# Attention and a gated feed-forward block on one core: three pairs of lag in place of two, gated tokens through DRAM, and another order at the end of a feed-forward phase

## The chip, the cores and the metric

One Trainium2 chip, of which the kernel uses one core. The engines of a core that matter here are TensorE (PE, matmuls), VectorE (DVE), ScalarE (ACT), GpSimd (POOL) and SyncE (SP), whose queue issues every DMA of this kernel. Each engine works through its own instructions in program order and waits for semaphores of the others. The metric is the device time of one execution in microseconds.

## The reference

```python
scores = np.matmul(z, z.transpose(0, 2, 1)) / S            # batch 4, S 3008, z 64 wide
attn = np.maximum(scores, 0.0) ** 2
x = (u * np.matmul(attn, v)).reshape(B * S, D)             # u, v 256 wide
rms = np.sqrt(np.mean(x * x, axis=-1, keepdims=True) + 1e-06)
xn = x / rms * rms_g
g, val = xn @ w_gate, xn @ w_val                           # 256 x 1536
return (g / (1 + np.exp(-g)) * val) @ w_out                # 1536 x 256
```

All of it is float32, and the kernel keeps that accuracy with matmuls of two halves (high and low) of each operand.

## The kernel before

The 3008 tokens of a batch are cut into 24 key tiles of 128 (the last of 64) and 6 query chunks of 512 (the last of 448). Two query chunks make a pair, so there are 3 pairs in a batch and 12 in all. For each pair p there are two phases:

- **Attention phase A(p)**, `phase_a`: 24 steps, one for each key tile. A step has up to 4 score matmuls (lines 366 and 367, high and low half of the moving operand), the relu on ACT (line 371) and the product with the score on DVE (line 373), which gives relu squared, then the high half H on ACT (line 389), the low half L on DVE (line 392) and 12 matmuls with v (lines 431, 432, 436). For some steps, the "squares" of `is_square`, ACT squares and DVE does nothing. Score tiles that a later pair needs transposed are stored as halves (line 411) and reloaded as T (line 344). At the end of the phase the gate multiplies the result by u (line 454), in place in the tile ux, into which u was loaded (line 446).
- **Feed-forward phase M(p)**, `phase_m` and `Unit`: 12 units. The gate and value products are computed as seven products of 3 matmuls (lines 616 to 618) with combined weights wu, which `load_unit` reloads from DRAM for every pair (line 600, a ring of 6 buffers). The unit's additions, silu and products follow on ACT and DVE (lines 623 to 710), the last of them, line 710, gives s. Its high and low halves hH (line 628, ACT) and hL (line 633, DVE) go into the output products py (lines 644, 645, 648), of which each unit has one for each of its two halves, `y(0)` and `y(1)`. Three such pieces of PE work wait at any time in the queue `pend`, and a unit takes two of them and adds two. `Unit.tail` ends a phase.

Between the two lie the norm of the gated tokens (`norm_jobs`, 23 small jobs) and the split of xn and its sums into halves (`split_jobs`, tiles xh and xl). The order of the phases was

```python
# before: A0 A1 M0 A2 M1 A3 M2 ... A11 M10 M11
```

Which other work runs beside a phase is set by a table: `at(phase, slot, fn)` puts a function into a slot (an attention phase has 24, one for each step; a feed-forward phase 36, three for each unit), `hook` calls it there, and `Beside.put` looks for the next slot with room on the engine. Such work is

- the weights, once: each third j is decoded on DVE and ACT (lines 142 to 153), combined in pieces of 128 columns on POOL (lines 124, 168, 169), and stored to DRAM as wc. j = 0 ran in A0, j = 1 in A1, j = 2 and half of w_out in M0;
- each batch b after the first (`plan_batch`): loads of z and v, high halves of v on ACT (line 301), low halves of v on POOL (line 312). It ran in M1, M4 and M7, before the batch's first attention phase;
- the moving operand of the next attention phase (`prep_mov`): a load of zT into a "raw" buffer (line 249), and its halves mh and ml on DVE (lines 254 and 255).

SP issues all DMAs in program order from one queue.

Of the kernel before, what the change touches and what calls it, by code (L numbers as in the profile page):

```python
# [19 lines left out]
P = 128  # L20
# [10 lines left out]
def kernel(  # L31
# [31 lines left out]
    LA = 2  # L63
    PIECE = 128
# [26 lines left out]
    misc = const.tile([P, 2 * P], F32, name="misc")  # L91
    g_sb, warm = misc[:, :ND], misc[:, ND:ND + 1]
# [80 lines left out]
    def prep_proj(j, pool, tags):  # L173
# [57 lines left out]
        "batch": ["raw", "mh0", "raw", "ml0", "mh1", "ml1"],  # L231
# [121 lines left out]
    def emit_s(p, i):  # L353
        b, c0 = where(p)[:2]
        kt = order(p)[i]
        todo = []
        for k in range(2):
# [10 lines left out]
            todo.append((k, n, ps))  # L368
        for k, n, ps in todo:
            a = att[p, i, k] = work.tile([P, CH], F32, tag="r", name="r", bufs=6)  # L370
            nc.scalar.activation(a[:, :n], ps[:, :n], AF.Relu)  # L371
            if not is_square(p, i, k):
                nc.vector.tensor_tensor(a[:, :n], ps[:, :n], a[:, :n], op=ALU.mult)  # L373

    copies = [0]

    def emit_l(p, i):
        b, c0 = where(p)[:2]
        kt = order(p)[i]
        for k in range(2):  # L380
# [61 lines left out]
    def load_u(p):  # L442
        t0, n2 = where(p)[2:]
        for d in range(ND):
            t = work.tile([P, PAIR], F32, tag=f"ux{d}", name=f"ux{d}")
            nc.sync.dma_start(out=t[:, :n2], in_=uT[d * P:(d + 1) * P, t0:t0 + n2])
            ux[p, d] = t
# [10 lines left out]
    def norm_jobs(p):  # L458
# [4 lines left out]
        small = misc[:, P:].rearrange("p (k a) -> p k a", a=PAIR // BLK)  # L463
# [100 lines left out]
    def split_jobs(p):  # L564
        n = where(p)[3] // 2
        last = p == NPAIR - 1
# [40 lines left out]
    class Unit:  # L607
# [108 lines left out]
        def tail(self, fills):  # L716

            fills = deque(fills)
            self.end0()
            if fills:  # L720
                fills.popleft()()
            self.end1()
            self.end2()
            pend.popleft()()
            if fills:
                fills.popleft()()
            self.end3()
            while pend:
                pend.popleft()()
# [87 lines left out]
    for p in range(NPAIR):  # L817
# [4 lines left out]
        for i in range(0, NK, 2):  # L822
            for k in range(2):
                if is_turned(p, i, k):
                    go = lambda p=p, i=i, k=k: load_turned(p, i, k)
                    if i < 8 and p > 1:
                        at(("M", p - 2), 3 * (NF - 2 if i < 6 else NF - 1) + 1, go)
                    else:
                        at(ph, max(i - 7, 0), go)
        if p:  # L830
            for f in range(ahead(p - 1)):
                at(ph, NK - 3 + f, lambda p=p, f=f: load_unit(p - 1, f))
        at(ph, 1 if p == 0 else (23 if p == 1 else 10), lambda p=p: load_u(p))
        if 0 < p < NPAIR:
            for i in range(NO):
                s = 19 + i * 4 // NO if p == 1 else i
                one = lambda p=p, i=i: splits(p - 1)[i][0]()
                two = lambda p=p, i=i: splits(p - 1)[i][1]()
                at(ph, s, one)
                at(ph, s + 1 if s < NK - 1 else s, two)  # L840

    def plan_batch(b):

        m = beside[b * NP - 2]
        todo = [prep_stat(b, c) for c in range(NC)] + [prep_v(b, g) for g in range(NK // 2)]
        done = []
        for k, (load, one, two) in enumerate(todo):
            if k == NC:
                m.put(norm_plan(b * NP - 1), 1)
# [10 lines left out]

    for p in range(1, NPAIR):

        m = beside[p - 1]
        if p % NP == NP - 1 and p < NPAIR - 1:
            continue
        h = m.put(norm_plan(p), 1)
        if p == NPAIR - 1:
            for i in range(NO):
                m.put([
                    ("a", 0.6, 0, lambda p=p, i=i: splits(p)[i][0]()),  # L870
                    ("d", 0.7, 0, lambda p=p, i=i: splits(p)[i][1]()),
                ], max(h, 18))
    for i, (e, cost, gap, fn) in enumerate(norm_plan(0)):
        at(("A", 1), 1 + i * 17 // 23 + (2 if i >= 8 else 0) - (1 if i < 8 else 0), fn)

    for p in range(1, NPAIR):

        for k in range(2):
            load, split, _ = prep_mov(p, k)
            if p > 1:  # L880
                m = beside[p - 2]
                at(m.phase, 3 * 9 + 1 + k, load)
                at(m.phase, 3 * 10 + 2 + k, split)
            else:
                at(("A", 0), NK - 4, load)
                at(("A", 0), NK - 1, split)
# [21 lines left out]
    tags_x = [f"xh{k}" for k in range(4)], [f"xl{k}" for k in range(4)]  # L908
    tags_m = ["mh0", "ml0", "mh1", "ml1"]

    def plan_part(part, phase, load_at, s):
# [6 lines left out]
    def plan_ends(ends, phase, s, gap=1):  # L918
        for k, fns in enumerate(ends):
            for fn in fns:  # L920
                at(phase, s + gap * k, fn)

    for j, ph, tags, s in ((0, ("A", 0), tags_x[0], 5), (1, ("A", 1), tags_x[1], 2)):
        parts, ends = prep_proj(j, moving, tags)
        for k, part in enumerate(parts):
            plan_part(part, ph, s + 2 * k - 2, s + 2 * k)
        plan_ends(ends, ph, s + 9)
# [81 lines left out]
```

## Time and profile before

| what | value |
|---|---|
| median of 3 runs | 2170.81 us (2168.62 to 2171.17) |
| the profiled execution | 2173.18 us |
| its span, first to last instruction | 2171.4 us |
| PE busy | 2066.8 us, 95% of the span |
| DVE busy | 1614.9 us, 74% |
| ACT busy | 1433.0 us, 66% |
| POOL busy | 207.9 us, 10% |
| granted clock of PE, mean | 0.98 |
| DMA | 295.85 MB, 136 GB/s |

Busy is the time in which an engine executes an instruction. A row of idle time names what ended it, the releaser: "PE ps L616 <- DVE s L710" is PE at line 616 standing until DVE's line 710 was done. The clock of PE has two levels, 1.2 and 2.4 GHz; a granted clock of 1.00 means 2.4 GHz throughout.

### The profile page before, as it was taken

Reading aid. Unit: us, or ns where it says so; the run is one execution under the profiler, and the core shown is the slowest. Engines: PE = TensorE matmul, PEld = TensorE weight load, DVE = VectorE, ACT = ScalarE, POOL = GpSimd, SP = SyncE. Lnnn points to the kernel's source line nnn. Section 1 sums busy time; section 2 is a strip of 40 time slices with the busy share of each in tenths; the row PEclk is TensorE's granted clock in tenths of the full one; section 3 lists DMA queues with packets and bytes.
Section 4 is the critical chain, followed back from the end, with each engine's and each line's share of the span. In section 5 each row is a group of like instructions: output and inputs, shape, how many; then the busy total and the mean of one; then the engine's idle time right before and its main releaser. Section 6 shows DMA issues by size and latency. Waiting matters only on the chain.

```text
span 2171.4 us, 27099 instructions
## 1 busy us (share of the span) xinstructions
PE 2066.8 (95%) x8968; PEld 1696.4 (78%) x8968; DVE 1614.9 (74%) x2661; ACT 1433.0 (66%) x2573; POOL 207.9 (10%) x376
## 2 busy tenths in 40 slices
PE   8898869998999999999899999999899999999999
PEld 7676657886888878787688778788688877878887
DVE  8898857677877677667778768757787767776765
ACT  7787536575965775656776775656596567565665
POOL 0635440022000000003000000001300000000000
PEclk9999979999999999999999999999999999999999
DMA  4405442251544544764254553495245445375342
GB/s 132 135 23 161 141 137 69 101 173 66 181 149 124 137 155 131 169 184 136 86 193 136 144 156 118 121 191 187 87 149 165 145 114 163 129 150 151 121 154 86
DMA packets 306829, 295.85 MB, mean 136 GB/s; under 512 B 195200, under 2 KB 232192, under 8 KB 306688
## 3 DMA queue, kind: packets, MB, share of 16 engines
q1 hardware_dynamic: 306688, 294.12, 45.3%
q8 instruction: 70, 1.15, 0.2%
q14 instruction: 71, 0.58, 0.1%
HBM read 178.46 MB, written 69.47 MB: 114 GB/s over the span
## 4 chain that ended last, share of the span: by engine, by line
PE 78%; issue 7%; DVE 7%; ACT 4%; POOL 4%; DMA 2%; POOLq 0%; DVEq 0%; SPq 0%; ACTq 0%
PE po L431 11%; PE po L432 11%; PE po L436 11%; PE ps L616 8%; PE ps L618 8%; PE ps L617 8%; PE py L648 4%; PE py L644 4%; PE py L645 4%; PE ps L367 4%; PE ps L366 4%; POOL vl L312 3%; DVE hL L633 1%; ACT r L371 1%; DVE L L392 1%
## 5 line engine op out<-in xcount | busy, mean ns | idle before, releaser
L431 PE MATMUL po<-H,vh 128*128 128x512 f32 (+1 forms) x1152 | 450.9, 391 | 7.8 <-ACT H L389 4.4
L432 PE MATMUL po<-H,vl 128*128 128x512 f32 (+1 forms) x1152 | 448.9, 390 | 0.0
L616 PE MATMUL ps<-xh,wu 128*128 128x512 f32 (+1 forms) x1008 | 398.0, 395 | 36.0 <-DVE s L710 19.8
L623 ACT COPY s<-ps 128x512 f32<-128x512 f32 (+1 forms) x432 | 249.4, 577 | 227.4 <-PE ps L618 227.4
L617 PE MATMUL ps<-xh,wu 128*128 128x512 f32 (+1 forms) x1008 | 392.3, 389 | 3.6 <-DMA wu<-wc 3.6
L618 PE MATMUL ps<-xl,wu 128*128 128x512 f32 (+1 forms) x1008 | 391.7, 389 | 0.0
L436 PE MATMUL po<-L,vh 128*128 128x512 f32 (+1 forms) x1104 | 340.4, 390 | 2.6 <-DVE L L392 2.4
L373 DVE TENSOR_TENSOR r<-ps,r 128x512 f32<-128x512 f32 x356 | 231.1, 680 | 141.0 <-ACT r L371 140.5
L628 ACT CAST hH<-s 128x512 fp32r<-128x512 f32 (+1 forms) x288 | 176.6, 613 | 238.2 <-DVE s L710 222.1
L371 ACT ACTIVATE r<-ps 128x512 f32<-128x512 f32 (+1 forms) x392 | 216.0, 598 | 141.0 <-PE ps L367 129.4
L392 DVE TENSOR_TENSOR L<-r,H 128x512 fp32r<-128x512 f32 x368 | 251.7, 696 | 45.5 <-ACT H L389 41.6
L633 DVE TENSOR_TENSOR hL<-s,hH 128x512 fp32r<-128x512 f32 (+1 forms) x288 | 198.4, 689 | 104.1 <-ACT hH L628 92.8
L431 PEld LDWEIGHTS po<-H,vh 128*128 128x128 f32 x1152 | 219.8, 191 | 56.0 <-ACT H L389 6.6
L616 PEld LDWEIGHTS ps<-xh,wu 128*128 128x128 f32 x1008 | 190.8, 189 | 89.0 <-DVE s L710 26.1
L432 PEld LDWEIGHTS po<-H,vl 128*128 128x128 f32 x1152 | 219.2, 190 | 42.4
L436 PEld LDWEIGHTS po<-L,vh 128*128 128x128 f32 x1104 | 208.3, 190 | 47.4 <-DVE L L392 8.3
L644 PE MATMUL py<-hH,woh 128*128 128x512 f32 (+1 forms) x576 | 226.2, 393 | 1.2 <-ACT hH L628 1.0
L645 PE MATMUL py<-hH,wol 128*128 128x512 f32 (+1 forms) x576 | 224.9, 390 | 0.0
L617 PEld LDWEIGHTS ps<-xh,wu 128*128 128x128 f32 x1008 | 191.2, 190 | 38.8 <-DMA wu<-wc 4.7
L618 PEld LDWEIGHTS ps<-xl,wu 128*128 128x128 f32 x1008 | 191.2, 190 | 37.0
L389 ACT CAST H<-r 128x512 fp32r<-128x512 f32 x356 | 217.4, 627 | 0.2 <-DVE r L373 0.2
L648 PE MATMUL py<-hL,woh 128*128 128x512 f32 (+1 forms) x576 | 180.1, 394 | 31.2 <-DVE hL L633 31.2
(82 smaller groups left out, 2790.3 us busy)
## 6 DMA issues: line engine op xcount, KB each, us to landing
wu<-wc SPq DMA_DIRECT2D x288, 448.0 KB, 3.9
kept<-halves SPq DMA_DIRECT2D x168, 256.0 KB, 2.0
raw<-in_v SPq DMA_DIRECT2D x44, 256.0 KB, 4.1
raw<-in_zT SPq DMA_DIRECT2D x38, 256.0 KB, 4.3
ux<-in_uT SPq DMA_DIRECT2D x16, 512.0 KB, 4.7
out_T<-y SPq DMA_DIRECT2D x32, 256.0 KB, 2.0
wc<-wohi SPq DMA_DIRECT2D x21, 256.0 KB, 2.4
wc<-wolo SPq DMA_DIRECT2D x21, 256.0 KB, 2.2
```

The source lines that it names most:

```text
L371: nc.scalar.activation(a[:, :n], ps[:, :n], AF.Relu)
L392: nc.vector.tensor_tensor(lo[:, :n], a[:, :n], f32(hi[:, :n]), op=ALU.subtract)
L431: nc.tensor.matmul(po[d][:, :n], wh[:, j, ds], hi[:, :n], start=(i == 0), stop=False)
L432: nc.tensor.matmul(po[d][:, :n], wl[:, j, ds], hi[:, :n], start=False, stop=(ends and lo is None))
L436: nc.tensor.matmul(po[d][:, :n], wh[:, j, ds], lo[:, :n], start=False, stop=ends)
L616: nc.tensor.matmul(ps[:, :n], wh[:, o, :], xh[:, :n], start=start, stop=False, skip_group_check=True)
L617: nc.tensor.matmul(ps[:, :n], wl[:, o, :], xh[:, :n], start=False, stop=False, skip_group_check=True)
L618: nc.tensor.matmul(ps[:, :n], wh[:, o, :], xl[:, :n], start=False, stop=stop, skip_group_check=True)
L623: nc.scalar.copy(s, ps[:, :self.n])
L644: nc.tensor.matmul(acc[h, d][:, :n], woh[:, f, ds], hi[:, :n], start=(f == 0), stop=False)
L645: nc.tensor.matmul(acc[h, d][:, :n], wol[:, f, ds], hi[:, :n], start=False, stop=False)
L648: nc.tensor.matmul(acc[h, d][:, :n], woh[:, f, ds], lo[:, :n], start=False, stop=(f == NF - 1))
```

## The change

- The order of the phases becomes A0 A1 A2 M0 A3 M1 ... A11 M8 M9 M10 M11 (`LAG = 3`).
- The gate leaves ux: four pieces of u are loaded in the last three steps of A(p) into buffers of other tiles, multiplied (line 475), stored to a DRAM tile xg (line 476), and loaded again by `load_x` (line 488) into ux, in step 9 of A(p+1) for most pairs.
- The preparation of all weights is spread over A0, A1 and A2. Its loads run 3 steps ahead instead of 2.
- `is_square` changes: 12, 12 and 6 steps' halves in pairs 0, 1 and 2, in place of 12, 24 and none.
- Batch preparation moves to M0, M3 and M6, and the norms and splits move with the order. The ring of buffers of batch loads begins with the four tiles of the moving operand.
- `emit_s` is cut into `s_product`, `s_relu` and `s_mult`, and `tail` puts these of the next pair's steps 0 and 1 between the last output products.

The core of the diff; cut are the plans of norms and splits, `load_u`, and the loop that calls the phases:

```diff
     raws = {
...
-        "batch": ["raw", "mh0", "raw", "ml0", "mh1", "ml1"],
+        "batch": ["mh0", "ml0", "mh1", "ml1", "raw", "raw"],
...
     def is_square(p, i, k):
-        if p == 0:
-            return (2 * i + k) % 4 == 1
-        return p == 1 and k == 1
+        return p < 3 and k == 1 and i % 4 in ((1, 3), (1, 3), (2,))[p] and not is_turned(p, i, k)
...
     def emit_gate(p, k):
+
         n = width(where(p)[1] + k)
-        cs = slice(k * CH, k * CH + n)
+        if p not in xg:
+            xg[p] = dram.tile([ND, P, PAIR], F32, tag=f"xg{p}", name=f"xg{p}")
         for d in range(ND):
-            x = ux[p, d]
-            nc.vector.tensor_tensor(x[:, cs], acc[k, d][:, :n], x[:, cs], op=ALU.mult)
+            x = us.pop((p, k, d))
+            nc.vector.tensor_tensor(x[:, :n], acc[k, d][:, :n], x[:, :n], op=ALU.mult)
+            nc.sync.dma_start(out=xg[p][d, :, k * CH:k * CH + n], in_=x[:, :n])
+
+    def load_x(p):
+        n2 = where(p)[3]
+        for d in range(ND):
+            t = ux[p, d] = work.tile([P, PAIR], F32, tag=f"ux{d}", name=f"ux{d}")
+            nc.sync.dma_start(out=t[:, :n2], in_=xg[p][d, :, :n2])
...
-        def tail(self, fills):
-
-            fills = deque(fills)
+        def tail(self, q=None):
+
             self.end0()
-            if fills:
-                fills.popleft()()
+            if q is not None:
+                s_product(q, 0)
             self.end1()
+            if q is not None:
+                s_relu(q, 0, 0)
             self.end2()
             pend.popleft()()
-            if fills:
-                fills.popleft()()
+            if q is not None:
+                s_relu(q, 0, 1)
+                s_mult(q, 0, 0)
             self.end3()
-            while pend:
-                pend.popleft()()
+            if q is not None:
+                s_mult(q, 0, 1)
+                emit_l(q, 0, (0,))
+            pend.popleft()()
+            if q is not None:
+                emit_s(q, 1)
+                emit_l(q, 0, (1,))
+            pend.popleft()()
+            assert not pend
...
+        at(ph, NK - 3, lambda p=p: load_u(p, [(0, 0)]))
+        at(ph, NK - 1, lambda p=p: load_u(p, [(0, 1), (1, 0), (1, 1)]))
...
-        m = beside[b * NP - 2]
+        m = beside[(b - 1) * NP]
...
+    def plan_part(part, g):
         load, upper, lower, split = part
-        at(phase, load_at, load)
-        at(phase, s, upper)
-        at(phase, s + 1, lower)
-        at(phase, s + 2, split)
...
+        at_step(g - 3, load)
+        at_step(g, upper)
+        at_step(g + 1, lower)
+        at_step(g + 2, split)
+
+    for j, steps, end in ((0, (5, 9, 13, 17), 26), (1, (24, 28, 32, 36), 39), (2, (40, 44, 48, 51), 54)):
+        parts, ends = prep_proj(j, moving, tags_w[j])
+        for g, part in zip(steps, parts):
+            plan_part(part, g)
+        for k, fns in zip((0, 1, 2, 3, 5, 7, 8, 10, 12), ends):
             for fn in fns:
-                at(phase, s + gap * k, fn)
...
+                at_step(end + k, fn)
+    for f, g in zip(range(0, NF, 2), (54, 57, 60, 63, 66, 69)):
+        plan_part(prep_wout(f), g)
```

How the order moves at three places. First DVE at the end of M1, before: s and r are the last unit's and the next attention phase's tiles, hL the low half that the output products wait for, py the outputs.

```order
L710 TENSOR_TENSOR s<-ps,s 128x512
L665 TENSOR_TENSOR s<-ps,s 128x512
L373 TENSOR_TENSOR r<-ps,r 128x512 x2
L633 TENSOR_TENSOR hL<-s,hH 128x512
L672 TENSOR_TENSOR s<-s 128x512
L373 TENSOR_TENSOR r<-ps,r 128x512 x2
L392 TENSOR_TENSOR L<-r,H 128x512 x2
L633 TENSOR_TENSOR hL<-s,hH 128x512
L656 COPY y<-py 128x512 x2
```

And after (line 661 is hL, 381 the score product, 406 L, 684 the copy of an output):

```order
L738 TENSOR_TENSOR s<-ps,s 128x512
L693 TENSOR_TENSOR s<-ps,s 128x512
L661 TENSOR_TENSOR hL<-s,hH 128x512
L700 TENSOR_TENSOR s<-s 128x512
L381 TENSOR_TENSOR r<-ps,r 128x512
L661 TENSOR_TENSOR hL<-s,hH 128x512
L381 TENSOR_TENSOR r<-ps,r 128x512
L406 TENSOR_TENSOR L<-r,H 128x512
L684 COPY y<-py 128x512
L381 TENSOR_TENSOR r<-ps,r 128x512 x2
L406 TENSOR_TENSOR L<-r,H 128x512
L684 COPY y<-py 128x512
```

The second hL now stands behind one score product, where it stood behind four and two L; the copies of the outputs lie between score products and L.

Second PE at the same place, before: the end of an output product, the scores of step 1 (lines 366 and 367), and the first of the last unit's two output products.

```order
L648 MATMUL py<-hL,woh 128x512 x2
L366 MATMUL ps<-mh,zst_4107 128x512
L367 MATMUL ps<-ml,zst_4107 128x512
L366 MATMUL ps<-mh,zst_4107 128x512
L367 MATMUL ps<-ml,zst_4107 128x512
L644 MATMUL py<-hH,woh 128x512
L645 MATMUL py<-hH,wol 128x512
L644 MATMUL py<-hH,woh 128x512
L645 MATMUL py<-hH,wol 128x512
L648 MATMUL py<-hL,woh 128x512 x2
```

And after:

```order
L676 MATMUL py<-hL,woh 128x512 x2
L366 MATMUL ps<-mh,zst_3370 128x512
L367 MATMUL ps<-ml,zst_3370 128x512
L366 MATMUL ps<-mh,zst_3370 128x512
L367 MATMUL ps<-ml,zst_3370 128x512
L672 MATMUL py<-hH,woh 128x512
L673 MATMUL py<-hH,wol 128x512
L672 MATMUL py<-hH,woh 128x512
L673 MATMUL py<-hH,wol 128x512
L676 MATMUL py<-hL,woh 128x512 x2
```

The scores of step 1 moved behind the first output product of the last unit, and lie between the two.

Third SP's queue of DMAs at the end of A4 and in the next feed-forward phase, before: stores of kept halves, then weights of all 12 units.

```order
L411 DMA kept_7223<-halves 128x1024
L411 DMA kept_7215<-halves 64x1024
L411 DMA kept_7223<-halves 64x1024
L600 DMA wu<-wc_80 128x896 x8
L600 DMA wu<-wc_81 128x896 x8
L600 DMA wu<-wc_82 128x896 x8
```

And after (line 628 loads weights, 465 a piece of u, 476 stores gated tokens):

```order
L425 DMA kept_6419<-halves 64x1024
L425 DMA kept_6427<-halves 64x1024
L628 DMA wu<-wc_80 128x896 x2
L465 DMA u<-in_uT 128x512
L628 DMA wu<-wc_80 128x896 x4
L465 DMA u<-in_uT 128x512 x3
L476 DMA xg_6700<-u 128x512 x2
L628 DMA wu<-wc_80 128x896 x2
L476 DMA xg_6700<-u 128x512 x2
L628 DMA wu<-wc_81 128x896 x8
L628 DMA wu<-wc_82 128x896 x8
```

The u pieces and the stores of the gated tokens now stand between the loads of the first weights; before, u was loaded in step 10 of the phase.

## Rows read from the trace of the kernel before

Names: ps scores or products in PSUM, po attention output, py feed-forward output, wu combined weights, s a unit's values, hL its low half, ml and vl low halves of the moving operand and of v, r relu and its square, H and L its halves.

**Rows 1.** The page, part 1: busy us (share of the span) xinstructions
```profile
PE 2066.8 (95%) x8968; PEld 1696.4 (78%) x8968; DVE 1614.9 (74%) x2661; ACT 1433.0 (66%) x2573; POOL 207.9 (10%) x376
```

**Rows 2.** Windows: us, busy of PE, PEld, DVE, ACT, POOL, PEclk, DMA, GB/s
```profile
5.50:197.00 191.50, 179.00 (x744) 140.87 (x745) 168.65 (x266) 150.31 (x279) 82.25 (x136) 0.99 0.34 106
197.00:334.80 137.80, 107.20 (x400) 81.88 (x399) 98.82 (x161) 64.97 (x120) 52.12 (x92) 0.87 0.41 133
334.80:421.60 86.80, 83.89 (x373) 71.62 (x372) 62.94 (x106) 56.49 (x108) 0.00 (x0) 0.96 0.23 72
421.60:515.10 93.50, 90.89 (x399) 74.24 (x398) 70.26 (x116) 62.29 (x115) 23.46 (x46) 1.00 0.45 150
...
1300.90:1391.70 90.80, 90.62 (x400) 74.35 (x400) 68.57 (x117) 53.34 (x97) 0.00 (x0) 1.00 0.44 127
```

**Rows 3.** Waits of PE, whole span: total us, times, longest
```profile
PE py L648 <- DVE hL L633: 31.2, 13, 3.1
```

**Rows 4.** Waits of PE in 197 to 334.8 us
```profile
PE ps L616 <- DVE s L710: 13.0, 6, 4.9
PE ps L616 <- DMA wu<-wc: 12.3, 2, 8.0
```

**Rows 5.** Timeline 874 to 881.5: start, us, engine line op, idle before and releaser
```profile
875.15 0.68 DVE L672 TENSOR_TENSOR s<-s 128x512 f32<-128x512 f32 x1
...
877.02 1.22 DVE L373 TENSOR_TENSOR r<-ps,r 128x512 f32<-128x512 f32 x2 [1.19 <-ACT r L371]
...
878.16 0.68 DVE L392 TENSOR_TENSOR L<-r,H 128x512 fp32r<-128x512 f32 x1
...
879.91 0.68 DVE L633 TENSOR_TENSOR hL<-s,hH 128x512 fp32r<-128x512 f32 x1
...
880.65 0.73 PE L648 MATMUL py<-hL,woh 128*128 128x512 f32 x2 [2.91 <-DVE hL L633]
```

**Rows 6.** Windows of 10 us behind two of the ten changes
```profile
340.00:350.00 10.00, 7.09 (x21) 5.49 (x20) 6.70 (x11) 6.79 (x12) 0.00 (x0) 0.66 0.41 158
1919.00:1929.00 10.00, 7.09 (x26) 5.88 (x26) 6.28 (x12) 7.00 (x13) 0.00 (x0) 0.83 0.42 160
```

**Rows 7.** Waits of DVE, whole span
```profile
DVE ml L255 <- POOL vl L312: 16.4, 6, 4.3
```

**Rows 8.** Timeline 504 to 521, a split on DVE
```profile
516.13 0.69 DVE L255 SCALAR_TENSOR_TENSOR ml<-raw,mh 128x512 fp32r<-128x512 f32 x1 [4.27 <-POOL vl L312]
```

**Rows 9.** Lines of DVE in 197 to 334.8: xcount | busy, mean ns | idle before
```profile
L145 DVE SCALAR_TENSOR_TENSOR wraw<-wraw,wt 128x512 uint32<-128x512 uint32 x7 | 5.0, 710 | 8.8 <-ACT w L142 5.2 <-ACT woh L142 3.7
...
L143 DVE TENSOR_SCALAR wt<-wraw 128x512 uint32<-128x512 uint32 x7 | 3.5, 505 | 0.0
...
L454 DVE TENSOR_TENSOR ux<-po,ux 128x512 f32<-128x512 f32 x4 | 2.7, 687 | 3.5 <-DMA ux<-in_uT 3.4
```

**Rows 10.** Window 150 to 195 us
```profile
150.00:195.00 45.00, 40.78 (x180) 33.29 (x179) 39.25 (x64) 36.56 (x68) 31.28 (x48) 1.00 0.39 115
```

**Rows 11.** Lines of DVE in 150 to 195 us
```profile
L392 DVE TENSOR_TENSOR L<-r,H 128x512 fp32r<-128x512 f32 x20 | 15.8, 804 | 2.6 <-ACT r L387 2.0 <-PE po L436 0.3 <-ACT H L389 0.2
L373 DVE TENSOR_TENSOR r<-ps,r 128x512 f32<-128x512 f32 x12 | 8.1, 676 | 0.2 <-ACT r L371 0.2
```

**Rows 12.** Lines of DVE in 540 to 609 us
```profile
L392 DVE TENSOR_TENSOR L<-r,H 128x512 fp32r<-128x512 f32 x36 | 24.4, 684 | 3.6 <-ACT H L389 3.6
```

**Rows 13.** Lines of POOL, whole span
```profile
L124 POOL TENSOR_TENSOR wolo<-w,wohi 128x128 fp32r<-128x128 f32 x60 | 36.2, 633 | 27.5 <-ACT wohi L195 10.3 <-issue 9.1 <-DMA wc<-wohi 7.9
```

**Rows 14.** DMA issues: out<-in, queue, kind, xcount, KB each, us to landing
```profile
ux<-in_uT SPq DMA_DIRECT2D x16, 512.0 KB, 4.7
out_T<-y SPq DMA_DIRECT2D x32, 256.0 KB, 2.0
```

**Rows 15.** Timeline 779 to 789, SP's queue and DVE
```profile
781.10 7.89 SPq L600 DMA_DIRECT2D wu<-wc  x2
...
787.42 1.28 DVE L454 TENSOR_TENSOR ux<-po,ux 128x512 f32<-128x512 f32 x2
```

More of the change, by code (lines that the diff above doesn't have):

```diff
@@ L825, with plan_splits, split_jobs_at @@
                     go = lambda p=p, i=i, k=k: load_turned(p, i, k)
-                    if i < 8 and p > 1:
-                        at(("M", p - 2), 3 * (NF - 2 if i < 6 else NF - 1) + 1, go)
+                    if i < 8 and p >= LAG:
+                        at(("M", p - LAG), 3 * (NF - 2 if i < 6 else NF - 1) + 1, go)
                     else:
                         at(ph, max(i - 7, 0), go)
[L830 to L840, printed above, removed]
+        if p >= LAG - 1:
+            for f in range(ahead(p - LAG + 1)):
+                at(ph, NK - 3 + f, lambda p=p, f=f: load_unit(p - LAG + 1, f))
+        at(ph, NK - 3, lambda p=p: load_u(p, [(0, 0)]))
+        at(ph, NK - 1, lambda p=p: load_u(p, [(0, 1), (1, 0), (1, 1)]))
+    def plan_splits(p, phase, slots):
+        for (one, two), s in zip(split_jobs_at(p), slots):
+            at(phase, s, one)
+            at(phase, s + 1 if s < NK - 1 else s, two)
+    def split_jobs_at(p):
+        return [
+            (lambda i=i: splits(p)[i][0](), lambda i=i: splits(p)[i][1]()) for i in range(NO)
+        ]
     def plan_batch(b):
-        m = beside[b * NP - 2]
+        m = beside[(b - 1) * NP]
         todo = [prep_stat(b, c) for c in range(NC)] + [prep_v(b, g) for g in range(NK // 2)]
@@ L847, in plan_batch @@
         for k, (load, one, two) in enumerate(todo):
-            if k == NC:
-                m.put(norm_plan(b * NP - 1), 1)
+            if k == NC and b == 1:
+                m.put(norm_plan(1), 1)
             s = max(3 * (k // 2) - 2, 0) + k % 2
@@ L859 @@
         plan_batch(b)
-    for p in range(1, NPAIR):
-        m = beside[p - 1]
[L864 to L874, printed above, removed]
+    at(("A", 1), 3, lambda: load_x(0))
+    for i, (e, cost, gap, fn) in enumerate(norm_plan(0)):
+        at(("A", 1), 5 + i * 15 // 23 + (2 if i >= 8 else 0), fn)
+    plan_splits(0, ("A", 2), [16, 17, 18, 19, 20, 21, 22])
+    at(("A", 2), NK - 1, lambda: load_x(1))
+    for p in range(1, NPAIR):
+        if 1 < p < NPAIR - 1:
+            at(("A", p + 1), 9, lambda p=p: load_x(p))
+        if p < NPAIR - 2:
+            plan_splits(p, ("A", p + 2), range(NO))
+        if p == 1:
+            continue
+        jobs_ = norm_plan(p)
+        m = beside[p - 1]
+        start = 1
+        if p % NP == 1:
+            early = 13
+            for i, (e, cost, gap, fn) in enumerate(jobs_[:early]):
+                at(("A", p + 1), 11 + i * 9 // early + (2 if i >= 8 else 0) + (1 if i >= 9 else 0), fn)
+            jobs_ = jobs_[early:]
+        elif p == NPAIR - 1:
+            at(m.phase, 0, lambda p=p: load_x(p))
+            start = 3
+        h = m.put(jobs_, start)
+        if p >= NPAIR - 2:
+            for one, two in split_jobs_at(p):
+                m.put([("a", 0.6, 0, one), ("d", 0.7, 0, two)], max(h, 15))
     for p in range(1, NPAIR):
@@ L884 @@
             else:
-                at(("A", 0), NK - 4, load)
-                at(("A", 0), NK - 1, split)
+                at(("A", p - 1), NK - 5, load)
+                at(("A", p - 1), NK - 1, split)
     first = {}
@@ L957 @@
         emit_l(0, 0)
-        phase_a(0)
-        for go in enter_a(1):
-            go()
-            pend.popleft()()
-        pend.popleft()()
-        phase_a(1)
+        for p in range(LAG):
+            phase_a(p)
+            if p + 1 < LAG:
+                for go in enter_a(p + 1):
+                    go()
+                    pend.popleft()()
+                pend.popleft()()
         prev = None
@@ L973 @@
                     load_unit(p + 1, f)
-        prev.tail([])
+        prev.tail()
         assert not jobs, jobs
```

81 lines of the change are left out of this document (40 added, 41 removed).

## Prediction, written before the changed kernel was run

> **What bounds the kernel now.** I read the page first: TensorE (PE) is busy for 95% of a span of 2171.4 us and VectorE (DVE) for 74% [rows 1]. So the time is PE's work plus the places in which PE stands. Then I cut the span at the first matmul of each phase and read busy time and granted clock per stretch, and after that asked for the waits of PE and of DVE. Where nothing is waited for, a matmul over 512 columns follows the last one after 0.227 us: the multiplication phase of pair 6 takes 90.8 us for 400 matmuls, with PE busy for 90.62 [rows 2] (the last row). Time is lost in three kinds of place:
>
> 1. The multiplication phase of pair 0 takes 137.8 us, with PE busy for 107.2 at a clock of 0.87 [rows 2] (the second row). It runs beside the preparation of the last third of the weights; PE waits there 13.0 us for DVE's last operation of a unit and 12.3 us, in two waits, for combined weights [rows 4].
> 2. Each of the ten changes from a multiplication phase to an attention phase. One wait is named there: the low half of the last unit (hL), made by DVE, 31.2 us in 13 waits, none over 3.1 [rows 3]. The timeline of one such tail shows why [rows 5]: the product of line 672 starts at 875.15, but the hL that needs it starts only at 879.91, behind two score multiplications and both L operations of the first attention step, since DVE works in program order. PE gets it at 880.65, after 2.91 us of standing. PE's clock then falls to half for some us: of the ten windows of 10 us behind these waits the first has a granted clock of 0.66 and the last 0.83 [rows 6], and what lacks to 1.00 adds up over the ten to 19.7 us at most.
> 3. The stretch ahead of each new batch: on DVE the split of the next moving operand (line 255) waits for GpSimd (POOL) to finish low halves of v, 16.4 us in 6 waits for the three batches [rows 7]. The operand comes through the raw buffer that POOL still reads [rows 8]: DVE stands 4.27 us.
>
> **The change part by part.** The sum is made against the profiled execution (2173.2 us, span 2171.4), which lies 2.4 above the median of the runs (2170.8).
>
> *Weights prepared in three attention phases and no multiplication phase.* The multiplication phase of pair 0 now has the batch preparation that pair 1's had, 93.5 us, and pair 1's has none, 90.8 [rows 2]. Before, the two took 137.8 + 93.5 = 231.3; after, 184.3: **−47**. Less if only the named waits went (13.0 + 12.3): −25.
>
> *What this puts into the first three attention phases.* They have 191.5 + 86.8 = 278.3 us, in which DVE is busy for 168.65 + 62.94 = 231.6, and the third has no POOL work at all [rows 2]. About 35 decoding operations of DVE at 0.50 to 0.71 us [rows 9] come in, 23 us; 6 score multiplications more, since squares go from 36 to 30, 4 us; and the price of POOL beside DVE. In a stretch of 45 us with 64 operations of DVE and 48 of POOL, POOL being busy for 31.28 [rows 10], an L operation took 804 ns and a score multiplication 676 [rows 11]; in a stretch without POOL the L operation took 684 [rows 12]. So 120 ns more for those that take both inputs from SBUF; if that is about half of the 64, 32 × 120 ns over 48 is some 70 to 80 ns per POOL operation. 84 come in: 6 us. Sum 265 of 278, 95%. In the first two phases DVE is busy for 88% and PE stands for 12.5 of 191.5 us [rows 2]; at the same share the third would stand 5.7, and I add 2 for the fuller DVE: **+8**. Bounds: −4 (loads a step earlier help the first phase) and +22.
>
> The Trainium skill has a rule that speaks against this part (SBUF — State Buffer, SBUF: two separate sides): GpSimd and VectorE share a port pair as an exclusive lock, so that a VectorE operation with two inputs in SBUF and a GpSimd operation that reads SBUF fully block one another. By it the sum would be that of the third rival. The trace shows a slowdown here, 120 ns for the L operation [rows 11, 12], and not the length of a whole POOL instruction, 633 ns [rows 13].
>
> *The tail.* On DVE hL of both halves now stands ahead of all but one score multiplication. In durations of [rows 5]: from the first score matmul on, add, hL, product, one score multiplication and hL, 5 × 0.6, and some 0.7 for casts that are waited for: ready at 3.7 us. PE needs it behind 24 matmuls (4 + 6 + 6 + 4 + 4), as many as before: 5.4 us. The wait ends: 31.2 less its three small ones, **−30**; and with it the low clock, for which I take **−15** of the 19.7, since part of those windows is the standing itself. Late next is the last copy of an output: DVE's twelfth operation there, done at 12 × 0.6 + 0.7 = 7.9 us, and PE wants that bank for the second pair of attention products, behind 36 matmuls, at 8.2. That margin is smaller than one operation; I put **+5** for the nine tails (0.5 each). Bounds for the tails in all: −17 and −50.
>
> *Batches.* Preparation moves to the multiplication phases of pairs 0, 3 and 6, which again lie right ahead of the batch's first attention, and the ring of buffers for it begins with the four of the moving operands (mh, ml), with raw last. In batches 2 and 3 the moving operands' loads then stand clear of POOL's last pieces: 5.5 us of DVE each [rows 7], **−11** (bound 0). In batch 1 the load waits for a raw buffer that POOL reads to the end, lands some 4 us later, and the split is in order on DVE ahead of the unit's additions: **+3** (0 to +8).
>
> *Gate through DRAM.* For each pair four loads of 256 KB in place of two of 512, four stores of 256 KB and two loads of 512. The DMA share is 0.44 in the undisturbed phase [rows 2], a load of 512 KB lands in 4.7 us and a store of 256 in 2.0 [rows 14], and the reload stands several steps ahead of its use: 0, with idle DMA engines as cover. The stores stand in SP's queue behind the gate, with weight loads behind them: 0, as those are needed three units later. The point to watch are the u pieces, which stand behind the weight loads that start at 781.10 and come up to 1.6 us later; 4.7 after that they are there, at 786 to 787.4. The gate starts at 787.42 [rows 15]. Just in time: 0, bounded by the fourth rival.
>
> **Sum**: −47 + 8 − 30 − 15 + 5 − 11 + 3 = −87: 2173.2 − 87 = 2086 on the profile's basis, less 2.4: **2084 us**.
>
> **Rivals.**
> *Tails half gone.* PE still stands at the nine tails, for the bank of an output that is copied late or for L of step 0, which now comes behind hL. For it: each operation put ahead pushes another back, and the margin above is 0.3 us. Against: what is late next is late by less than an operation of 0.7. Half of 45 stays: 2084 + 22 = 2106.
> *Upper bounds.* All of the clock back, −4 in the first phases, tails with no new wait: 2084 − 5 − 12 − 5 = 2062.
> *Three attention phases bound by DVE.* If each of the 84 POOL pieces held DVE for its whole length, about 0.6 us [rows 13], that would be 50 us in place of 6: 309 us of DVE. Without any idleness the three phases take 309, at the 92% of the forecast (265 of 286) 336; in the middle 322, 36 beyond the forecast: 2120. This is what the named page's rule would do here. Against it are the 804 ns of [rows 11].
> *Slower: u lands late.* DVE is in order, so a gate that waits for its DMA holds the next unit's additions, and PE follows. Once it is seen: in the multiplication phase of pair 0 the gate waited 3.4 us for u [rows 9]. Price: 12 × what the gate waits. It decides above 87/12 = 7.3 us each; at 9.4, two landings of 4.7, it is 2084 + 113 = 2197. Against: the queue ahead of the pieces is one landing long in [rows 15], not three.
>
> **Numbers.** Forecast 0.55, with a range of its own from 2068 to 2100; tails half gone 0.22; bound by DVE 0.15; u late 0.04; upper bounds 0.04. From **2060 to 2118** lie 8 in 10: outside are the last rival, most of the third and the edges. 0.2% is 4.3 us, about what a measurement of this kernel tells from no change. Between the cases at 2120 and 2197 lies little: faster 0.95, same 0.02, slower 0.03.
>
> **What would show it.** Right: the multiplication phase of pair 0 takes 91 to 100 us; no wait of PE for hL at the tails and a clock of 1.00 behind them; the third attention phase takes 87 to 95 us with DVE busy for over 85%; DVE waits for POOL or a load of raw ahead of batch 1 alone. Wrong: L operations over 1 us on the mean in the third attention phase; gate operations that wait for u; PE standing for a copy of y at the start of the attention products; any one new wait of over 20 us in all.

## The result and the profile after

The changed kernel takes 2100.2 us (median of 4 runs, 2098.6 to 2102.8) against 2171.0 before: a ratio of 0.9677, with a 95% interval of 0.9660 to 0.9694. The forecast was 2084, the range 2060 to 2118. So the direction and most of the size came as forecast, and 16 us of the gain are missing. Of the signs that the prediction named, one failed: M0 takes 111.8 us and not 91 to 100. The profiled execution has a span of 2101.0 us, 70.4 less than before. On the page after, the engines' busy time answers to [rows 1]:

```profile
PE 2041.3 (97%) x8968; PEld 1687.7 (80%) x8968; DVE 1618.2 (77%) x2668; ACT 1426.3 (68%) x2566; POOL 219.9 (10%) x376
```

The phases again from first matmul to first matmul, as in [rows 2] (us, busy time and instructions of PE, PEld, DVE, ACT and POOL, PE's clock, DMA share, GB/s): the three first attention phases, M0, A3, M1 and A5.

```profile
5.50:286.90 281.40, 263.36 (x1116) 212.22 (x1116) 259.98 (x408) 207.37 (x387) 139.97 (x220) 0.98 0.39 119
286.90:398.70 111.80, 97.19 (x398) 78.62 (x399) 79.19 (x130) 64.33 (x119) 27.16 (x55) 0.91 0.50 166
398.70:483.60 84.90, 84.84 (x373) 69.69 (x372) 74.49 (x121) 75.27 (x126) 1.49 (x3) 1.00 0.50 173
483.60:574.30 90.70, 90.54 (x399) 74.35 (x398) 68.05 (x117) 53.10 (x97) 0.00 (x0) 1.00 0.51 148
...
739.90:814.20 74.30, 70.28 (x311) 59.85 (x310) 49.17 (x90) 43.97 (x80) 0.00 (x0) 0.95 0.67 167
```

A3 and M1 have no hole left. M0 and A5 have: 111.8 us with PE busy for 97.2, and 74.3 with 70.3. Cut in the same way over both traces, the 70.4 us come from these phases:

| phases | before | after | difference |
|---|---|---|---|
| A0, A1, A2 | 278.5 | 281.4 | +2.9 |
| M0, M1 | 231.2 | 202.5 | −28.7 |
| A3, A6, A9 | 283.1 | 254.2 | −28.9 |
| A4, A7, A10 | 250.3 | 238.2 | −12.1 |
| A5, A8, A11 | 216.8 | 219.5 | +2.7 |
| M2 to M11 | 906.0 | 899.7 | −6.3 |

The waits of PE over the whole span (total us, times, longest) tell what stands in place of [rows 3] and [rows 4]:

```profile
PE ps L644 <- DMA wu<-wc: 12.0, 2, 10.5
PE po L445 <- ACT H L403: 10.5, 3, 3.8
PE po L450 <- DVE L L406: 7.6, 8, 1.8
...
PE ps L645 <- DMA wu<-wc: 3.0, 2, 2.0
...
PE ps L644 <- DVE s L738: 1.0, 1, 1.0
PE po L445 <- DVE u L475: 0.9, 2, 0.5
```

The wait for hL, 31.2 us before, is gone. New are one wait of 10.5 us for weights and three of up to 3.8 for H, and these two are what the forecast had not seen. The wait for L, 2.4 us before, is 7.6, all of it in the three first attention phases. The gate (line 475) cost PE 0.9 us in two waits, and none of them was for u.

**The tail.** The timeline at the end of M2, to be read against [rows 5]:

```profile
741.43 0.66 DVE L700 TENSOR_TENSOR s<-s 128x480 f32<-128x480 f32 x1
...
742.00 0.69 DVE L381 TENSOR_TENSOR r<-ps,r 128x512 f32<-128x512 f32 x1
...
742.75 0.66 DVE L661 TENSOR_TENSOR hL<-s,hH 128x480 fp32r<-128x480 f32 x1
...
745.10 0.59 PE L676 MATMUL py<-hL,woh 128*128 128x480 f32 x2
...
747.35 0.66 DVE L684 COPY y<-py 128x480 f32<-128x480 f32 x1
...
748.18 0.37 PE L445 MATMUL po<-H,vh 128*128 128x448 f32 x1
```

hL starts 1.3 us after the product, where it took 4.8 before, and is done 1.7 us before PE uses it. The last copy of y is done at 748.01, 0.17 us before the last of these attention products starts: the thin margin of the prediction (0.3 us) held. And the clock stays at 1.00 behind the tails, where [rows 6] had 0.66 and 0.83; a window behind the tail of M7:

```profile
1589.00:1599.00 10.00, 10.00 (x46) 8.26 (x45) 8.47 (x14) 9.82 (x18) 0.00 (x0) 1.00 0.52 180
```

**The end of M0.** Here POOL, SP's queue, DVE and PE, in order of time:

```profile
375.40 3.48 POOL L313 TENSOR_TENSOR vl<-raw,vh 128x128 fp32r<-128x128 f32 x8 [3.01 <-ACT vh L302]
378.90 4.31 SPq L250 DMA_DIRECT2D raw<-in_zT  x2
381.64 0.43 DVE L255 TENSOR_SCALAR mh<-raw 128x512 fp32r<-128x512 f32 x1 [5.96 <-DMA raw<-in_zT]
...
383.26 0.91 SPq L628 DMA_DIRECT2D wu<-wc  x2
...
386.83 0.80 PE L644 MATMUL ps<-xh,wu 128*128 128x512 f32 x1 [10.50 <-DMA wu<-wc]
```

The load of the moving operand waits for POOL, which reads the raw buffer until 378.88. Behind that load in SP's queue stand the weights of unit 11, and they go out at 383.26. PE stands for 10.5 us, and its next matmuls take 0.80 us in place of 0.39.

**A5.** SP's queue, ACT and PE:

```profile
763.71 13.18 SPq L345 DMA_TRANSPOSE T<-kept  x6
776.95 1.06 SPq L482 DMA_DIRECT2D ux<-xg  x2
782.32 0.63 ACT L504 ACTIVATE q<-ux 128x512 f32<-128x512 f32 x1 [7.46 <-DMA ux<-xg]
...
784.75 0.80 PE L445 MATMUL po<-H,vh 128*128 128x512 f32 x1 [3.66 <-ACT H L403]
```

The reload of the gated tokens is in step 9, but transposing loads stand ahead of it in the queue, and it is issued only at 776.95. The norm begins in step 11: ACT waits 7.46 us for its first operand, with the casts of H queued behind it, and PE stands for 3.66 us. A8 and A11 show the same waits (ACT 6.99 and 7.71 us, PE 3.1 and 3.8). In A5 the granted clock was 0.54 from 784 to 791; behind the wait of A8 it stayed at 1.00, and A8 is the shortest of the three (71.5 us against 74.3 and 73.7). The window of A5:

```profile
784.00:791.00 7.00, 6.25 (x17) 5.24 (x18) 5.58 (x10) 4.91 (x10) 0.00 (x0) 0.54 0.68 139
```

### The profile page after: what moved, and what is told of

Same layout as the page of the kernel before. It is cut to its first block, busy times and chain, and to the rows that moved or that the text cites. A ratio compares the mean times of both kernels' runs of the same rounds, so it can differ in the third digit from the quotient of the medians.

```text
span 2101.0 us, 27215 instructions
## 1 busy us (share of the span) xinstructions
PE 2041.3 (97%) x8968; PEld 1687.7 (80%) x8968; DVE 1618.2 (77%) x2668; ACT 1426.3 (68%) x2566; POOL 219.9 (10%) x376
## 4 chain that ended last, share of the span: by engine, by line
PE 81%; DVE 7%; issue 4%; ACT 3%; DMA 3%; POOL 1%; SPq 0%; DVEq 0%; ACTq 0%; POOLq 0%
PE po L445 11%; PE po L446 10%; PE po L450 10%; PE ps L644 10%; PE ps L645 9%; PE ps L646 9%; PE py L672 5%; PE py L673 5%; PE py L676 5%; PE ps L367 4%; PE ps L366 3%; DVE L L406 2%; DVE r L381 1%; POOL vl L313 1%; DMA ux<-xg 1%
## 5 line engine op out<-in xcount | busy, mean ns | idle before, releaser
L445 PE MATMUL po<-H,vh 128*128 128x512 f32 (+1 forms) x1152 | 452.1, 392 | 17.8 <-ACT H L403 10.5
L381 DVE TENSOR_TENSOR r<-ps,r 128x512 f32<-128x512 f32 (+1 forms) x363 | 235.5, 679 | 94.0 <-ACT r L374 93.1
L406 DVE TENSOR_TENSOR L<-r,H 128x512 fp32r<-128x512 f32 x368 | 256.6, 710 | 35.2 <-ACT H L403 32.1
L445 PEld LDWEIGHTS po<-H,vh 128*128 128x128 f32 x1152 | 219.0, 190 | 70.4 <-ACT H L403 13.1
L403 ACT CAST H<-r 128x512 fp32r<-128x512 f32 (+1 forms) x363 | 221.9, 631 | 5.1 <-DVE r L381 5.1
L313 POOL TENSOR_TENSOR vl<-raw,vh 128x128 fp32r<-128x128 f32 x144 | 75.5, 560 | 1022.7 <-ACT vh L302 1022.7
```

What stands on the lines that cost most here:

```text
L403: nc.scalar.copy(hi[:, :n], a[:, :n])
L406: nc.vector.tensor_tensor(lo[:, :n], a[:, :n], f32(hi[:, :n]), op=ALU.subtract)
L445: nc.tensor.matmul(po[d][:, :n], wh[:, j, ds], hi[:, :n], start=(i == 0), stop=False)
```

## The experiments

Each is the changed kernel with one edit unless it says otherwise; its time stands against 2100.2. The ratios to before of ahead3, ringA, woutm0, defer, oldsq and piece256 have intervals that overlap the changed kernel's (0.9660 to 0.9694), so none of these six differs from it by more than the noise, and what they teach is read from their traces. In the diffs, "..." stands for lines that are left out.

**The tail, both ways.** oldtail puts `tail` of before back; newtail is the kernel before with the new `tail` alone.

```diff
...
-                prev.tail(p + LAG)
+                prev.tail(enter_a(p + LAG))
...
```

> The changed kernel with the tail of before: hL of the last unit stands behind the score products and L of step 0 again. Theory: at each of nine tails PE stands for 3 us and then has a low clock for some us, 5 to 5.5 us each: 2145 to 2150, with a wait of PE for hL of 26 to 28 us. Rival: most of what the attention phases gained came from elsewhere (the batch order, the norm and splits that moved): 2115 to 2130.

> The kernel before with the new tail and nothing else. Theory: the ten tails lose 5 us each less: 2118 to 2126, with no wait of PE for hL at the tails and a granted clock of 1.00 behind most of them. Rival: ahead of each batch the splits wait for POOL as before, and at the three tails there PE stands for ml or s instead; at the others half of the wait moves to the copy of the outputs: 2140 to 2150.

Measured: oldtail 2142.4 (2136.9 to 2150.2), 42 more; newtail 2121.7, ratio 0.9783 (0.9768 to 0.9799), 47 less than the 2168.5 of before measured beside it. The first line is a wait of PE in oldtail, the next two are waits of PE in newtail, and the last two are windows of newtail over A4 and A5, where before had 84.6 and 72.0 us.

```profile
PE py L676 <- DVE hL L661: 27.3, 9, 3.1
```

```profile
PE py L659 <- ACT hH L643: 6.8, 3, 2.3
...
PE ps L368 <- DVE ml L255: 2.7, 3, 0.9
```

```profile
683.20:761.60 78.40, 77.61 (x341) 63.32 (x340) 56.46 (x90) 65.02 (x108) 0.00 (x0) 1.00 0.55 160
...
852.30:920.50 68.20, 67.88 (x310) 57.63 (x310) 45.37 (x74) 42.28 (x76) 0.00 (x0) 1.00 0.82 178
```

Ten tails gave 47 us, 4.7 each, and nine taken back cost 42, 4.7 each. The new tail is 42 to 47 of the 71 us that the whole change brought. Both edits exchange the whole tail, so that the order on PE and ACT moves with that on DVE; no run changes the order of DVE alone. The rival of oldtail falls, though its time is also 2.6 us below its theory's range and its four runs scatter over 13 us. Of newtail's rival the mechanism came in part: at the three tails ahead of a new batch PE stood for 2.3 us each for the high half hH and 0.9 for ml. Its price did not come, as the time lies within the theory's range.

**The norm three steps later.**

```diff
-                at(("A", p + 1), 11 + i * 9 // early + (2 if i >= 8 else 0) + (1 if i >= 9 else 0), fn)
+                at(("A", p + 1), 14 + i * 7 // early + (2 if i >= 8 else 0) + (1 if i >= 9 else 0), fn)
```

> The changed kernel with the norm of pairs 4, 7 and 10 begun in step 14 of the attention phase instead of step 11. Theory: the gated tokens land 5 to 7 us after their load is issued, the norm's first job on ACT waits for them, and the casts of H queue behind it in ACT's order. Some 9 us later they are there: the three waits of PE for H (10.5 us in all) and the low clock behind them go, A5, A8 and A11 take 67 to 69 us in place of 71.5 to 74.3, the whole 2084 to 2089. Rival: the norm's jobs now crowd the last steps of the phase, and what is gained is lost there: 2096 to 2102.

Measured: 2082.9, ratio to before 0.960 (0.9584 to 0.9616, clear of the changed kernel's 0.9677): 17 us less. The wait for H is not among its waits any more, and A5 takes 67.8 us. A window of 69 us around it:

```profile
739.00:808.00 69.00, 68.66 (x317) 58.90 (x316) 49.09 (x83) 44.07 (x80) 0.00 (x0) 1.00 0.79 181
```

A8 and A11 take 67.8 us as well. The theory holds, with its number.

**The end of M0, in three ways.** ahead3 loads the weights of pair 0 three units ahead; ringA gives the last v pieces of batch 1 other buffers; m0end lets three jobs share a slot of ACT in M0, so that v is done earlier, and puts the operand's load and split two slots later, behind the weights.

```diff
-        return 3 if p else 2
+        return 3
```

> The changed kernel with one number changed: the weights of pair 0 are loaded three units ahead, as for the other pairs, instead of two. Theory: at the end of M0 the load of the moving operand waits in SP's queue for POOL, and the weights of unit 11 wait behind it, which is PE's wait of 10.5 us. With the weights ahead of it in the queue that wait is gone: M0 goes from 111.8 to 99 to 103 us, the whole to 2088 to 2092. Rival: DVE's own wait for that operand (5.96 us, in order ahead of the unit's additions) is what holds PE, and the weights only come last: M0 stays at 105 to 109, the whole at 2094 to 2098.

```diff
+        "batch1": ["mh0", "ml0", "mh1", "ml1", "raw", "raw"] * 2 + ['mh0', 'raw', 'ml0', 'raw', 'mh1', 'ml1'],
...
```

> The changed kernel with another order of buffers for the last six loads of v of batch 1: raw goes to the second and fourth of them instead of the last two, mh and ml take the rest. Theory: DVE's split at the end of M0 waits for a load that waits for POOL's last piece but one; with raw read two and four pieces earlier the load goes out 4 to 8 us earlier, and PE's wait at the end of M0 (10.5 us and a low clock behind it) shrinks to 3 to 6: 2091 to 2096. Rival: the split of the second half now waits for POOL's last piece in mh and ml themselves, and PE stands at the first scores of A3 instead: 2099 to 2106.

```diff
-                (e, h): (0.75 if e == "d" else 1.35 if h % 3 == 2 else 0.0)
+                (e, h): (0.75 if e == "d" else (1.95 if p == 0 else 1.35) if h % 3 == 2 else 0.0)
...
-                at(m.phase, 3 * 9 + 1 + k, load)
-                at(m.phase, 3 * 10 + 2 + k, split)
+                at(m.phase, 3 * 9 + 1 + k + (2 if p == LAG else 0), load)
+                at(m.phase, 3 * 10 + 2 + k + (2 if p == LAG else 0), split)
```

> The changed kernel with two things at the end of M0: three jobs of batch 1 instead of two may share a slot of ACT, so that v is done eight slots earlier, and the load and split of the moving operand of pair 3 stand two slots later, behind the weights of unit 11. Theory: both waits that the run with weights three units ahead showed to lie over one another (PE for the weights behind the held load, DVE for the load itself) go: no wait of PE over 2 us in the second half of M0, M0 at 97 to 102 us in place of 111.8, the whole 2086 to 2092. Rival: ACT, fuller in these slots, is late with the units' values and PE waits for s, or the later split is late for A3: 2095 to 2103.

Measured: ahead3 2103.5, ringA 2104.3, m0end 2089.1 (ratio 0.9630, 0.9614 to 0.9646). The waits of PE of ahead3 from 286 to 400 us:

```profile
PE ps L644 <- DVE s L738: 6.9, 2, 5.9
PE ps L644 <- ACT s L651: 5.5, 2, 5.3
```

The wait for weights at the end is gone, and 5.9 us for DVE's s took its place: DVE stands for the operand, with the unit's product queued behind. The other 5.3 us are at the start of M0, where ACT's copy of a unit's values comes late; in that run the u pieces, the reload and the batch loads stand behind one more pair of weight loads, and ACT, in order, stands for one of these loads:

```profile
304.47 0.62 ACT L278 CAST zst<-raw 128x512 fp32r<-128x512 f32 x1 [7.27 <-DMA raw<-in_zT]
```

M0 took 113.9 us and missed the ranges of the theory and of the rival. So my theory was half of it: two waits lie over one another, and the queue's is only the longer. In ringA M0 shrank to 106.1 us, but A3 grew to 89.3, since the split of the second half then waited 4.9 us for POOL; that is the rival. m0end takes both away: the operand's load goes out at 362.28, behind the weights, and DVE does not wait for it. Its rows for SP and DVE, then M0 as a window, 96.5 us in place of 111.8:

```profile
353.65 8.27 SPq L628 DMA_DIRECT2D wu<-wc  x4
362.28 3.38 SPq L250 DMA_DIRECT2D raw<-in_zT  x2
...
380.84 0.42 DVE L255 TENSOR_SCALAR mh<-raw 128x512 fp32r<-128x512 f32 x1
```

```profile
287.10:383.60 96.50, 93.67 (x398) 75.95 (x399) 79.19 (x130) 64.05 (x119) 29.76 (x56) 0.96 0.56 191
```

**The start of M0.** In the changed kernel PE waits 3.5 us there for weights (1.53 and 1.99). Stores of combined weights wait for POOL in SP's queue until 281.1 us, the first weights behind them. woutm0 prepares the last third of w_out in M0; defer puts the store of S4 into M0.

```diff
...
+    for k, f in enumerate((8, 10)):
+        for fn, s in zip(prep_wout(f), (3 * k, 3 * k + 3, 3 * k + 4, 3 * k + 5)):
+            at(("M", 0), s, fn)
```

> The changed kernel with the last third of w_out (rows of units 8 to 11) prepared in the first eight slots of M0 instead of the last steps of A2. Theory: at the end of A2 POOL is behind (busy 49.98 of 52 us), the stores of combined weights wait for it in SP's queue, and the first weights and u pieces of M0 behind them: 16 POOL pieces less before the last store let it go some 10 us earlier, and the 3.7 us of PE's waits for wu at the start of M0 and the low clock behind them end: M0 down by 5 to 8 us, A2 by 2 for its waits for L, the whole 2090 to 2096. Rival: the preparation in M0 costs as much there as it freed, as in the kernel before: 2099 to 2106.

```diff
...
+                if j == 2 and o == S4:
+                    at(("M", 0), 1, store)
+                else:
+                    store()
```

> The changed kernel with one pair of stores (the last combined weight, S4) moved from step 18 of A2 to the second slot of M0. Theory: this store waits for POOL till 281.1 us in SP's queue, and the first weights and u pieces behind it come late: without it they go out some 8 us earlier, PE's waits of 3.7 us at the start of M0 and the low clock behind them end, M0 is 5 to 7 us shorter, the whole 2093 to 2096. Rival: the buffers of these weights come free no earlier, so that the wait stays: 2099 to 2103.

Measured: woutm0 2105.1, defer 2099.8. In woutm0 the last store still waited until 280.05: the POOL pieces that I moved stood behind that store in POOL's order, so nothing was freed; the time is that of the rival, but not for its reason. In defer the first weights went out at 272.3 and PE's wait for them ended, but the next pair of weights, and three of the u pieces behind it, still went out only at 286: in the queue this pair waits, by the profile, for POOL's last pieces of w_out (line 170). PE waited 4.7 us for ACT's copies instead, in two waits, and both times the copies queue behind an operation for which ACT waits, first 2.96 us for w_out from DVE, then, in the row below, for keys of the next batch:

```profile
297.08 0.62 ACT L284 CAST zst<-raw 128x512 fp32r<-128x512 f32 x1 [4.44 <-DMA raw<-in_zT]
```

No run takes all of these away. What the start of M0 costs stays an estimate: some 6 us, the 96.5 us of M0 in m0end less the 90.3 of M3, which in the changed kernel prepares a batch too.

**DVE and POOL in the first three phases.** oldsq has the squares of before; piece256 gives POOL pieces of 256 columns.

```diff
-    PIECE = 128
+    PIECE = 256
```

> The changed kernel with the squares of before (12, 24 and none in A0, A1 and A2 instead of 12, 12 and 6). Theory: DVE bounds the three phases at 92% busy, ACT has room; 12 score products less in A1 and 6 more in A2 leave DVE 4 us less in the sum, but A2, where POOL works most, gets 4 us more: the three phases take 281 to 287 in place of 281.4, the whole 2099 to 2107. Rival: in A1 the squares were what ACT was late with (its two operations each, 24 times), so that the old table costs more: over 2110.

> The changed kernel with POOL's work in pieces of 256 columns instead of 128: half as many instructions, each twice as long, in the weights and in the low halves of v. Theory: a DVE operation that meets POOL is slowed (822 ns against 685 for an L operation), whatever the piece: L beside POOL stays at 780 to 860 ns on the mean and under 1.1 us at most, and the time is 2094 to 2106. Rival: a POOL instruction holds DVE for its whole length, so that pieces of over 1 us hold it for longer: L beside POOL takes over 1.1 us on the mean, single ones 1.7 or more, and the three first phases take 10 us longer or more: over 2110.

Measured: oldsq 2100.2 (2094.3 to 2101.8), no difference; piece256 2105.2 (2104.0 to 2108.2). The lines of DVE in the part of A2 where POOL is busy for 49.98 of 52 us, in the changed kernel (234 to 286 us), then in a stretch of A3 without POOL (400 to 480), then in piece256 (234 to 290):

```profile
L406 DVE TENSOR_TENSOR L<-r,H 128x512 fp32r<-128x512 f32 x14 | 10.4, 744 | 0.0
...
L406 DVE TENSOR_TENSOR L<-r,H 128x448 fp32r<-128x448 f32 x11 | 9.5, 863 | 0.0
```

```profile
L406 DVE TENSOR_TENSOR L<-r,H 128x512 fp32r<-128x512 f32 x40 | 27.2, 685 | 3.7 <-ACT H L403 3.6
```

```profile
L406 DVE TENSOR_TENSOR L<-r,H 128x512 fp32r<-128x512 f32 x15 | 11.8, 790 | 0.0
L406 DVE TENSOR_TENSOR L<-r,H 128x448 fp32r<-128x448 f32 x12 | 11.5, 956 | 0.0
```

Taking all L operations over 512 columns of the changed kernel that lie beside POOL for over nine tenths of their time: 48, 822 ns on the mean, 1000 at most, against 685 for the 400 without POOL. In piece256 the mean POOL instruction is 891 ns instead of 618, and those L take 889 ns on the mean, 1229 at most. So both ranges for the mean are missed, and by the rival's further; the time is within the theory's. The mechanism is nearer the rival's, as single operations show. Four rows of A2 in the changed kernel:

```profile
275.83 0.68 DVE L381 TENSOR_TENSOR r<-ps,r 128x512 f32<-128x512 f32 x1
276.31 0.40 POOL L170 TENSOR_TENSOR wol<-wraw 128x128 fp32r<-128x128 f32 x1
276.44 0.83 DVE L406 TENSOR_TENSOR L<-r,H 128x512 fp32r<-128x512 f32 x1
...
276.67 0.91 POOL L169 TENSOR_TENSOR wraw<-wraw,woh 128x128 f32<-128x128 f32 x1
```

The score product, beside which POOL's line 169 has run since 275.33, keeps its 0.68 us. L starts while a POOL instruction has 0.27 us left, and takes 0.14 us longer than its 0.685. The POOL instruction that starts during L ends 0.31 us after L and takes 0.91 us, where the same line takes 0.46 alone. It is so for nearly every L over 512 columns that starts beside a running POOL instruction: it takes 0.685 us plus what that instruction still had to run, less 0.135 us (nothing more where less than 0.135 was left). To within 0.02 us this gives 53 of the 54 in the changed kernel and all 41 in piece256. So L does wait for the POOL instruction under way, but for its rest only: 0.14 us on the mean and 0.32 at most in the changed kernel, 0.22 and 0.54 in piece256. And the means of 618 and 891 ns contain POOL's own waits for DVE: where no DVE operation lies beside it, an instruction takes 0.40 to 0.47 us in pieces of 128, and 0.72 to 0.74 in the four such of piece256.

**The two that helped, together.** best has norm14, m0end and defer; two has norm14 and m0end.

> The changed kernel with three edits together: the norm of pairs 4, 7 and 10 from step 14, the end of M0 as in the run before last, the S4 store deferred. Theory: they lie in different places, so that their gains add: 17 us (measured for the norm) and 8 to 14 and 4 to 7 us: 2063 to 2073. Rival: they share waits, or one of the two in M0 gives nothing: 2074 to 2084.

> The changed kernel with the norm from step 14 and the new end of M0, and the S4 store where the change put it. Theory: the deferred store gave nothing by itself (2099.8 against 2100.2), so these two edits carry the whole gain: 2100 - 17 - 11 = 2072, between 2068 and 2074, like the run with all three (2070.3). Rival: behind the other two edits the store at the start of M0 counts after all: 2075 to 2079.

Measured: best 2070.3, two 2070.0 (2067.4 to 2070.5), ratio to before 0.9540 (0.9524 to 0.9556). The gains add: 17 + 11 = 28 of the 30 us. two is 30 us faster than the changed kernel, and the deferred store of best gave nothing beside the two others. Its largest waits of PE follow; but for 3.9 of the 5.9 us for H, they lie in the first three phases:

```profile
PE po L450 <- DVE L L406: 8.3, 9, 1.8
PE po L445 <- DVE H L410: 5.9, 8, 1.7
PE ps L366 <- DVE zst L282: 5.6, 1, 5.6
PE ps L366 <- DVE mh L255: 5.3, 2, 4.8
```

## Why the prediction was right, and 16 us off

- *Tails, −30 and −15 and +5.* Right in mechanism, a little small: 47 us for ten tails in newtail, 42 for nine in oldtail, against 40 forecast. The wait for hL went as a whole, the clock behind it came back (1.00 in the window above and in newtail's two), and no copy of y took its place, so the +5 was not needed.
- *The first three phases, +8.* With the one tail that A2 no longer has ahead of it (some 4.7 of gain) the forecast was a growth of 3 us, and 2.9 came. DVE is busy for 260.0 of 281.4 us, 92%, where I had 265 of 286. The rival bound by DVE falls in its price: the squares of before gave no difference, and L beside POOL took 822 ns. Its mechanism does not fall. The rule of the Trainium skill (SBUF — State Buffer, SBUF: two separate sides), by which one side fully blocks the other for a whole instruction, agrees with these traces instruction by instruction: the score product, with one input in PSUM, did not slow, and L with two in SBUF waited for the rest of the POOL instruction under way. I had read the 120 ns of [rows 11] as evidence against the rule, and that step was wrong: the kernel before shows the same wait, in all 40 L that start beside a running POOL instruction. The size came right since I took it from rows. The rival's 0.6 us for each piece was too much, because the 633 ns of [rows 13] contain POOL's own waits (alone these instructions take 0.46 us) and an L meets on the mean only part of one.
- *M0 and M1, −47.* This term failed: −28.7, where −47 and the +3 for batch 1 make −44. M1 came as forecast, 90.7 us. The step that failed was to take M0 at the 93.5 us that M1 had taken, with +3 (0 to +8) for batch 1: 96.5, against 111.8. I had seen that the operand's load waits for POOL and that the unit's additions queue behind the split on DVE. I had not asked what is queued behind that load in SP, which is the weights of the last unit, loaded for pair 0 only two units ahead. And the +3 was too small by itself: without the queue's wait PE still stood for 5.9 us behind the split (ahead3). With both gone M0 takes 96.5 us (m0end), so the end of M0 makes up the whole 15 us of the miss in the traces; between the medians it is 11. The start costs some 6 us more (estimate above). The rule that I had followed on DVE, I did not follow on the queue.
- *Gate through DRAM, 0.* The worry I had, late u, did not come: no gate waited for it. The term I set at nothing cost 17 us (norm14): "the reload stands several steps ahead of its use" is true of its place in the order, two steps, and not of its time, since transposes in the queue ahead of it took 13 us. This is the rival "u lands late" with another load: its mechanism, an engine in order behind an operand that is late, at three places instead of twelve and on ACT instead of DVE.
- *Batches, −11.* A3, A6 and A9 gave 28.9, of which three tails are 14, and M4 and M7 5.4 more: nearer 20 than 11. The trace of newtail agrees: there, with the new tail and the old batch order, the three take 268.6 us against 254.2, and PE's waits for hH and ml at their tails (6.8 and 2.7 us) are not among the changed kernel's behind A2. But no run took the batch order alone, so its share is read from two traces and not shown by an experiment.
- *Together*: forecast −87; 17 us were lost to the late reload and 15 in M0, and some 7 from the tails and 9 from the batches were added: −87 + 32 − 16 = −71, against −70.4 in the profiled execution. That the sum is only 16 us off is in part luck, as misses of 32 and 16 us went opposite ways.

## What to carry to other kernels

Where an engine is in order, an operation that the critical engine wants soon should not stand behind ones it wants later; here the new order of a dozen operations at each phase change (on DVE, and with it on PE and ACT) was worth some six tenths of a large change. When data takes a way through DRAM, ask for each load not how many steps ahead it stands but when the queue will issue it, and what else stands ahead of it and behind it there. And when one of two waits that lie over one another is taken away alone, nothing is gained: look at the second before calling the first innocent. Last, a mean over many operations can hide a block: compare single operations with what runs beside them before calling it a mere slowdown.

## What was not expected of the hardware

Beside POOL, DVE slowed only in operations that read SBUF alone, with one input as with two. The profiled execution of the changed kernel, mean of operations over 512 columns without POOL and with POOL beside them for over nine tenths of their time: L 685 and 822 ns, hL (line 661) 693 and 884, the one-input decoding of line 152 418 and 679 (four of them). Those that read a bank of PSUM did not change: the score product (line 381) 686 and 680, the additions of lines 693 and 738 688 and 690 to 691. I had expected it of two inputs alone. Not every operation within SBUF slows: the transposes of lines 512 and 551 kept their 704 ns (700 to 714 in three). And the price grows with the length of POOL's instruction, +137 ns for L in pieces of 128 columns and +204 in pieces of 256, since it is the rest of the instruction that L meets (the experiment piece256). The one-input decoding in 234 to 286 us:

```profile
L152 DVE TENSOR_SCALAR wt<-wraw 128x512 uint32<-128x512 uint32 x4 | 2.7, 684 | 0.0
```
